# k^T v head by head in two runs of four chunks, with four slots for x^T k in borrowed space

## Chip, cores, metric

One core of one Trainium2 chip. The metric is the time of one execution in device microseconds (us). The kernel before takes 1626.18 us (median of six runs, 1625.86 to 1627.21).

## The reference

Two layers of linear attention (A) and two of a bilinear feed-forward block (B), in turn, each on a layer-normed x and added to x. x is 2048 x 1024 in bf16, with 32 heads of 32 columns. Only A matters here:

```python
q, k, v = split(x @ wqkv)                          # x is layer-normed
pq, pk = phi(q), phi(k)
kv  = einsum("bhsd,bhse->bhde", pk, v)             # one 32x32 block per head
num = einsum("bhqd,bhde->bhqe", pq, kv)
den = einsum("bhqd,bhd->bhq", pq, pk.sum(s)) + 1e-6
out = (num / den) @ wo
```

The kernel never forms v. Because kv = pk^T (x Wv), it computes G = x^T pk, an array of 1024 x 1024 in eight chunks of 128 rows ("x^T k"), and then, head by head, the 32x32 blocks of Wv^T G ("k^T v" in the kernel's words). From those blocks and wo it makes one matrix M, so that the layer's output is pq M.

## The kernel before

Chunk m of G is made in PSUM by 32 full matmuls (128x128 weights, 512 columns), ScalarE copies it to a slot in SBUF, and then 32 small matmuls, one per head, add that chunk's share to the 32 blocks in one PSUM bank. There are two slots, used in turn:

```python
Gs = [GL[:, (2 + i) * D:(3 + i) * D] for i in range(2)]

def both(ps, lhsT, rhs, start, stop):              # L199; L202 after the change
    for n in range(2):
        nc.tensor.matmul(out=ps[:, n, :], lhsT=lhsT, rhs=rhs[:, n * NB:(n + 1) * NB], ...)

def g_unit(m):                                     # x^T k, chunk m
    def run():
        for n in range(2):
            if n == 0 or m == KD - 1:
                ps = mm_tile()
            for t in range(NT):
                nc.tensor.matmul(out=ps[:, n, :], lhsT=XN[:, t, m * P:(m + 1) * P],         # L291
                                 rhs=PK[:, t, n * NB:(n + 1) * NB], start=(t == 0), stop=(t == NT - 1))
            if m == KD - 1:                        # the last chunk is copied by halves
                nc.scalar.copy(out=Gs[m % 2][:, n * NB:(n + 1) * NB], in_=ps[:, n, :])      # L294
        if m < KD - 1:
            nc.scalar.copy(out=Gs[m % 2], in_=flat(ps))                                     # L296

def kv_unit(m):                                    # k^T v, chunk m: 32 matmuls of 128x32 by 128x32
    def run():
        ...
        for h in range(2):
            for j in range(4):
                for r in range(4):
                    a = (4 * h + r) * P + j * DH
                    nc.tensor.matmul(out=acc[0][DH * r:DH * r + DH, h, j, :], lhsT=wkv[:, m, a:a + DH],
                                     rhs=Gs[m % 2][:, a:a + DH], ..., tile_position=(0, DH * r))   # L310
        if m == KD - 1:
            nc.vector.tensor_copy(out=KVb[:], in_=acc[0][:])
```

The units stand in one hand-made order; `d` is the division of one tile of q on VectorE (about 4.3 us each), `q` the q matmuls of one tile (16 full matmuls):

```python
do([g[0], g[1], z_sum, kv[0]] + d(0) + [g[2], kv[1]] + d(1, 2) + [g[3], kv[2]] + d(3) + [q[0]] + d(4))
do([g[4], kv[3]] + d(5, 6) + [q[1], g[5], kv[4]] + d(7))
load_o(0)
load_o(1)
do(d(8) + [q[2], g[6], kv[5]] + d(9, 10) + [q[3]] + d(11) + [q[4]] + d(12) + [g[7], kv[6], kv[7], q[5]])
last_q_with_m(later)
```

`last_q_with_m` makes the last two q tiles and, among their matmuls, the four quarters of M (`quarter`, L334: 16 matmuls of 32x32 weights and 512 columns). Each quarter needs KVb, a part of wo, and free PSUM banks; VectorE and ScalarE take its results out (`take`). The quarters stand eight full matmuls apart.

## Time and profile before

The first lines are those of the page for the kernel before: span, busy time, granted clock of TensorE (PE) in 40 slices, and the chain of waits that ended last.

```profile
span 1624.7 us, 18711 instructions
...
PE 1620.1 (100%) x8129; PEld 735.3 (45%) x8129; DVE 609.4 (38%) x895; ACT 287.3 (18%) x389; POOL 54.5 (3%) x136
...
PEclk9999999999999999999999999999999999999999
...
PE 100%; ACT 0%; DVE 0%; issue 0%
```

PE is the chain almost from end to end, at full clock (a mean of 1.000 granted); the ACT in it is one copy of 0.59 us in each attention layer, which comes up again below. A saving anywhere else is worth nothing unless PE waits for it. "Busy 100%" also hides what is at stake here: a full matmul's record is 0.38 us long and overlaps the next one's, so PE counts as busy through the small gaps between groups. Those gaps are read from starts, not from busy time. A full matmul starts every 0.2158 us (448 of them take 96.69 us in the chain).

Next, PE's timeline of the kernel before, around the first chunk of k^T v and then at the end of k^T v in the first layer. Columns: start, duration, engine, line, operation, output and inputs, shapes, count, and in brackets idle time before and who ended it.

```profile
104.46 0.59 PE L199 MATMUL ps<-W,ones 128*128 128x512 bf16 x2
104.98 0.38 PE L310 MATMUL kv<-GL,W 128*32 128x32 bf16 x32
105.29 7.08 PE L291 MATMUL ps<-R,R 128*128 128x512 bf16 x32
112.30 0.38 PE L310 MATMUL kv<-GL,W 128*32 128x32 bf16 x32
...
166.16 0.53 PE L310 MATMUL kv<-GL,W 128*32 128x32 bf16 x48
166.90 0.28 PE L310 MATMUL kv<-GL,W 128*32 128x32 bf16 x16 [0.21 <-ACT GL L294]
167.11 3.63 PE L199 MATMUL ps<-W,xT 128*128 128x512 bf16 x16
```

I use one measure throughout, worked out from the starts of single matmuls in the trace: the **extra time** of a trip to small matmuls and back is the start of the first full matmul after it, minus the start of the last one before it, minus 0.2158 us. For the first chunk that is 105.290 - 104.673 - 0.216 = 0.401 us. The small matmuls fill 0.200 us of it, four per 25 ns (one for each column tile, 3 to 4 ns apart; only the second four start 40 ns after the first). The other 0.20 us is going in (0.093) and out (0.108).

At the end of k^T v, chunks 6 and 7 form one trip, and the second half of chunk 7 waits for ScalarE's copy: 1.044 us extra. The chain of waits of the kernel before (start, length, what) has that copy in it:

```profile
166.24 0.02 issue
166.27 0.59 ACT GL L294
166.86 0.04 issue
166.90 0.28 PE kv L310 x16
```

Some records are missing from traces (one full matmul in about 50, in some of the profiles below); I put back one spacing where that is plain.

| per attention layer, before | us |
|---|---|
| six single chunks, 0.401 each | 2.41 |
| chunks 6 and 7 with the wait | 1.04 |
| k^T v, extra time in all | 3.45 |
| four quarters of M, 0.461 each | 1.84 |

### The profile page before, as it was taken

The numbers are of one execution on the slowest core, as the hardware profiler recorded it, in microseconds if no ns is written. First come the engines' busy times: TensorE is split into PE (matmuls) and PEld (weight loads), VectorE is DVE, ScalarE is ACT, GpSimd is POOL, SyncE is SP. The second block draws the span as 40 slices with busy tenths as digits, with TensorE's granted clock in tenths as the row PEclk, the third lists the DMA queues.
The fourth block names the chain that finished last, engine by engine and source line by source line (L and its number), as shares of the span: only waits on it lengthen the run. The fifth ranks groups of instructions, "written<-read, shape, count | busy, mean of one in ns | idle before, by whom it ended". The sixth has DMA issues, their size and how long they took to land.

```text
span 1624.7 us, 18711 instructions
## 1 busy us (share of the span) xinstructions
PE 1620.1 (100%) x8129; PEld 735.3 (45%) x8129; DVE 609.4 (38%) x895; ACT 287.3 (18%) x389; POOL 54.5 (3%) x136
## 2 busy tenths in 40 slices
PE   9999999999999999999999999999999999999999
PEld 4444444444444444444444444444444444444444
DVE  6789853212311321243245798432123113211111
ACT  5533201101110110011045222011011101101110
POOL 2100000000000000010000000000000000000000
PEclk9999999999999999999999999999999999999999
DMA  7325856511550452142420358555235406521400
GB/s 236 57 71 105 234 162 175 162 52 53 165 171 0 139 160 90 52 156 63 91 55 1 78 104 243 151 170 162 71 96 173 134 20 172 165 66 65 156 0 26
DMA packets 235937, 182.87 MB, mean 113 GB/s; under 512 B 101456, under 2 KB 216656, under 8 KB 235856
## 3 DMA queue, kind: packets, MB, share of 16 engines
q1 hardware_dynamic: 235856, 181.69, 39.2%
q8 instruction: 63, 1.03, 0.3%
q14 instruction: 18, 0.15, 0.0%
HBM read 153.09 MB, written 4.19 MB: 97 GB/s over the span
## 4 chain that ended last, share of the span: by engine, by line
PE 100%; ACT 0%; DVE 0%; issue 0%
PE ps L523 48%; PE ps L199 44%; PE ps L291 7%; PE ps L550 1%; PE kv L310 0%; PE ps L169 0%; PE pm L334 0%; PE pt L406 0%; ACT GL L294 0%; DVE xT L409 0%; DVE X L531 0%; DVE xT L164 0%; PE ps L334 0%
## 5 line engine op out<-in xcount | busy, mean ns | idle before, releaser
L523 PE MATMUL ps<-xT,R 128*128 128x512 bf16 x2432 | 528.5, 379 | 0.0
L523 PEld LDWEIGHTS <-R 128*128 128x128 bf16 x2432 | 238.0, 98 | 286.9
L527 DVE TENSOR_TENSOR R<-gs,ps 128x512 bf16<-128x512 f32 x224 | 153.8, 687 | 533.6 <-ACT gs L526 533.6
L526 ACT COPY gs<-ps 128x512 f32<-128x512 f32 x224 | 131.0, 585 | 1040.4 <-PE ps L523 1040.4
L199 PEld LDWEIGHTS <-R 128*128 128x128 bf16 x1736 | 169.9, 98 | 204.8
L523 PE MATMUL ps<-xT,W 128*128 128x512 bf16 x1152 | 251.6, 379 | 0.0
L199 PEld LDWEIGHTS <-xT 128*128 128x128 bf16 x1536 | 148.7, 98 | 178.9 <-issue 1.8
L199 PE MATMUL ps<-W,xT 128*128 128x512 bf16 x1024 | 225.3, 380 | 0.3 <-DVE xT L409 0.3
L523 PEld LDWEIGHTS <-W 128*128 128x128 bf16 x1152 | 112.7, 98 | 136.0
L199 PE MATMUL ps<-W,R 128*128 128x512 bf16 x744 | 170.7, 379 | 0.0
L531 DVE TENSOR_TENSOR X<-X,ps 128x1024 bf16<-128x1024 bf16 (+3 forms) x34 | 39.4, 1158 | 335.8 <-PE ps L199 326.1
L291 PE MATMUL ps<-R,R 128*128 128x512 bf16 x512 | 112.8, 379 | 0.0
L199 PE MATMUL ps<-PQ,R 128*128 128x512 bf16 x496 | 112.1, 379 | 0.0
L199 PE MATMUL ps<-R,xT 128*128 128x512 bf16 x512 | 110.8, 379 | 0.0
L204 ACT ACTIVATE e<-ps 128x1024 bf16<-128x1024 f32 x56 | 57.3, 1024 | 145.5 <-PE ps L199 145.5
L178 DVE BATCH_NORM_STATS2 st<-X 128x6 f32<-128x512 bf16 x128 | 81.9, 681 | 1.9 <-DMA X<-in_A_x_dram 1.8
L291 PEld LDWEIGHTS <-R 128*128 128x128 bf16 x512 | 49.8, 98 | 59.6
L182 POOL TENSOR_SCALAR ve<-mv 128x1 f32<-128x1 f32 x64 | 16.7, 260 | 1330.4 <-DVE mv L180 1330.4
L199 PE MATMUL ps<-GL,R 128*128 128x512 bf16 x248 | 58.6, 379 | 0.0
L199 PE MATMUL ps<-xT,R 128*128 128x512 bf16 x248 | 58.6, 379 | 0.0
L377 DVE TENSOR_TENSOR X<-X,ps 128x1024 bf16<-128x1024 bf16 x32 | 38.6, 1212 | 26.6 <-PE ps L199 26.6
L189 DVE TENSOR_SCALAR R<-X,mv,rstd 128x1024 bf16<-128x1024 bf16 x64 | 33.9, 542 | 23.9 <-POOL rstd L184 23.9
(64 smaller groups left out, 474.5 us busy)
## 6 DMA issues: line engine op xcount, KB each, us to landing
R<-in_B_w_gate_dram SPq DMA_DIRECT2D x38, 1024.0 KB, 5.4
R<-in_B_w_up_dram SPq DMA_DIRECT2D x38, 1024.0 KB, 7.4
W<-in_B_w_gate_dram SPq DMA_DIRECT2D x18, 1024.0 KB, 5.6
W<-in_B_w_up_dram SPq DMA_DIRECT2D x18, 1024.0 KB, 7.4
W<-in_A_wqkv_dram SPq DMA_DIRECT2D x10, 1024.0 KB, 5.9
W<-in_B_w_down_dram SPq DMA_DIRECT2D x6, 1024.0 KB, 11.5
PQ<-in_B_w_down_dram SPq DMA_DIRECT2D x4, 1024.0 KB, 7.9
X<-in_A_x_dram SPq DMA_DIRECT2D x15, 256.0 KB, 5.4
```

What stands on the lines that cost most here:

```text
L178: nc.vector.bn_stats(out=st[:, c, :], in_=X[:, t, c * NB:(c + 1) * NB])
L182: nc.gpsimd.tensor_scalar(out=ve[:], in0=mv[:, 1:2], scalar1=1e-5, scalar2=None, op0=ALU.add)
L189: nc.vector.tensor_scalar(out=dst, in0=X[:, t, :], scalar1=mv[:, 0:1], scalar2=rstd[:], op0=ALU.subtract, op1=ALU.mult)
L199: nc.tensor.matmul(out=ps[:, n, :], lhsT=lhsT, rhs=rhs[:, n * NB:(n + 1) * NB], start=start, stop=stop)
L204: nc.scalar.activation(out=e[:], in_=flat(ps), func=ACT.Exp, **sc)
L291: nc.tensor.matmul(out=ps[:, n, :], lhsT=XN[:, t, m * P:(m + 1) * P], rhs=PK[:, t, n * NB:(n + 1) * NB], start=(t == 0), stop=(t == NT - 1))
L377: nc.vector.tensor_tensor(out=X[:, t, :], in0=X[:, t, :], in1=flat(ps), op=ALU.add)
L523: nc.tensor.matmul(out=ps[:, n, :], lhsT=w[:, k, j * P:(j + 1) * P], rhs=xT[g % 2][:, k, :], start=(k == 0), stop=(k == KD - 1))
L526: nc.scalar.copy(out=gs[:], in_=ps[:, 0, :])
L527: nc.vector.tensor_tensor(out=hT[:, f, :], in0=gs[:], in1=ps[:, 1, :], op=ALU.mult)
L531: nc.vector.tensor_tensor(out=X[:, t, a:b], in0=X[:, t, a:b], in1=ps, op=ALU.add)
L550: nc.tensor.matmul(out=ps[:, 0, 0:b - a], lhsT=hT[:, f, tl * P:(tl + 1) * P], rhs=wd[f][:, a:b], start=(f == 0), stop=(f == KF - 1))
```

## The change

Its intent: gather the eight chunks, seven trips, into two trips, so that TensorE leaves its full matmuls less often, and put the second run behind a q tile, so that the last copy is covered. That takes four slots in place of two. They come from a new tile G3, from a quarter of W3 that wo fills later, and from pq[7], which is free by then but belongs to wo's second half, whose last slice can then be loaded only after the second run. x^T k also shares one lhsT between two banks, and the quarters of M move by some q matmuls.

```diff
+    G3 = const.tile([P, D], BF16, tag="G3", name="G3")
+    Gs = [GL[:, 2 * D:3 * D], GL[:, 3 * D:4 * D], G3[:], W3[:, 3 * D:4 * D]]
+    Gs += Gs[0:3] + [pq[7]]
 ... g_unit
-                for n in range(2): ...
+                ps = mm_tile()
+                for t in range(NT):
+                    both(ps, XN[:, t, m * P:(m + 1) * P], PK[:, t, :], t == 0, t == NT - 1)
+                if m == 4:
+                    kv_unit(0)()
+                nc.scalar.copy(out=Gs[m], in_=flat(ps))
 ... kv_unit(i)
+                for m in range(4 * i, 4 * i + 4):       # the 32 small matmuls as before
 ... last_q_with_m: q steps of two matmuls each, round the four quarters
-            quarter(0,0) steps(0,0,4) quarter(0,1) steps(0,4,8) quarter(1,0) steps(1,0,4) quarter(1,1) steps(1,4,8)
+            steps(0,0,2) quarter(0,0) steps(0,2,5) quarter(0,1) steps(0,5,8) steps(1,0,1)
+            quarter(1,0) steps(1,1,5) quarter(1,1) steps(1,5,8)
 ... order
-        load_o(0)
-        load_o(1)
-        do(... [g[7], kv[6], kv[7], q[5]])
+        load_o(0, 0, 4)
+        load_o(1, 0, 3)
+        do(... [g[7], q[5], kv_unit(1)])
+        load_o(1, 3, 4)
```

More of the change, by code (lines that the diff above doesn't have):

```diff
@@ L87 @@
     zhl = W3[:, 0:D]
-    Gs = [GL[:, (2 + i) * D:(3 + i) * D] for i in range(2)]
+    G3 = const.tile([P, D], BF16, tag="G3", name="G3")
+    Gs = [GL[:, 2 * D:3 * D], GL[:, 3 * D:4 * D], G3[:], W3[:, 3 * D:4 * D]]
+    Gs += Gs[0:3] + [pq[7]]
     ring = [rows(R2[:, i * KD * NB:(i + 1) * KD * NB], NB) for i in range(4)]
@@ L121, in load_q, with load_o @@
             load(wq[:, a:a + 4, :], wqkv_v[:, a:a + 4, 0:D])
-    def load_o(h):
+    def load_o(h, a, b):
         for r in range(4):
-            load(wo[h][DH * r:DH * r + DH, :, :], wo_v[h, r])
+            load(wo[h][DH * r:DH * r + DH, a:b, :], wo_v[h, r, :, a:b, :])
     def load_gu(i):
@@ L286, in run @@
             def run():
-                for n in range(2):
-                    if n == 0 or m == KD - 1:
-                        ps = mm_tile()
-                    for t in range(NT):
-                        nc.tensor.matmul(out=ps[:, n, :], lhsT=XN[:, t, m * P:(m + 1) * P],
-                                         rhs=PK[:, t, n * NB:(n + 1) * NB], start=(t == 0), stop=(t == NT - 1))
-                    if m == KD - 1:
-                        nc.scalar.copy(out=Gs[m % 2][:, n * NB:(n + 1) * NB], in_=ps[:, n, :])
@@ L295, in run, with kv_unit @@
-                if m < KD - 1:
-                    nc.scalar.copy(out=Gs[m % 2], in_=flat(ps))
+                ps = mm_tile()
[4 more added lines that the diff above has]
+                nc.scalar.copy(out=Gs[m], in_=flat(ps))
             return run
         acc = []
-        def kv_unit(m):
+        def kv_unit(i):
             def run():
-                if m == 0:
+                if i == 0:
@@ L305, in run @@
                     acc[:] = [psum.tile([P, 2, 4, DH], F32, tag="kv0", bufs=1, name="kv")]
-                for h in range(2):
-                    for j in range(4):
-                        for r in range(4):
-                            a = (4 * h + r) * P + j * DH
-                            nc.tensor.matmul(out=acc[0][DH * r:DH * r + DH, h, j, :], lhsT=wkv[:, m, a:a + DH],
-                                             rhs=Gs[m % 2][:, a:a + DH], start=(m == 0 and h == 0 and j == 0),
-                                             stop=(m == KD - 1), tile_position=(0, DH * r), skip_group_check=True)
@@ L313, in run @@
-                if m == KD - 1:
+                for m in range(4 * i, 4 * i + 4):
+                    for h in range(2):
+                        for j in range(4):
+                            for r in range(4):
+                                a = (4 * h + r) * P + j * DH
+                                nc.tensor.matmul(out=acc[0][DH * r:DH * r + DH, h, j, :], lhsT=wkv[:, m, a:a + DH],
+                                                 rhs=Gs[m][:, a:a + DH], start=(m == 0 and h == 0 and j == 0),
+                                                 stop=(m == KD - 1), tile_position=(0, DH * r), skip_group_check=True)
@@ L314, in run @@
+                if i == 1:
                     nc.vector.tensor_copy(out=KVb[:], in_=acc[0][:])
@@ L346, in last_q_with_m @@
             dve, act = nc.vector.tensor_copy, nc.scalar.copy
+            steps(0, 0, 2)
             take = quarter(0, 0, qs[1])
@@ L350, in last_q_with_m @@
             take(act, 2)
-            steps(0, 0, 4)
+            steps(0, 2, 5)
             take = quarter(0, 1, wide)
@@ L355, in last_q_with_m @@
             take(act, 2)
-            steps(0, 4, 8)
+            steps(0, 5, 8)
+            steps(1, 0, 1)
             take = quarter(1, 0, wide)
@@ L361, in last_q_with_m @@
             phi(qs[0], q_slot(14), scale_of(14), later)
-            steps(1, 0, 4)
+            steps(1, 1, 5)
             take = quarter(1, 1, wide)
@@ L367, in last_q_with_m @@
             do(later)
-            steps(1, 4, 8)
+            steps(1, 5, 8)
             phi(qs[1], q_slot(15), scale_of(15))
@@ L481, in d @@
             return [div_unit(t) for t in ts]
-        g, kv, q = ([f(i) for i in range(KD)] for f in (g_unit, kv_unit, lambda i: q_unit(8 + i)))
+        g, q = ([f(i) for i in range(KD)] for f in (g_unit, lambda i: q_unit(8 + i)))
         later = []
         q[5] = q_unit(13, later)
-        do([g[0], g[1], z_sum, kv[0]] + d(0) + [g[2], kv[1]] + d(1, 2) + [g[3], kv[2]] + d(3) + [q[0]] + d(4))
-        do([g[4], kv[3]] + d(5, 6) + [q[1], g[5], kv[4]] + d(7))
-        load_o(0)
-        load_o(1)
-        do(d(8) + [q[2], g[6], kv[5]] + d(9, 10) + [q[3]] + d(11) + [q[4]] + d(12) + [g[7], kv[6], kv[7], q[5]])
+        do([g[0], g[1], z_sum] + d(0) + [g[2]] + d(1, 2) + [g[3]] + d(3) + [q[0]] + d(4))
+        do([g[4]] + d(5, 6) + [q[1], g[5]] + d(7))
+        load_o(0, 0, 4)
+        load_o(1, 0, 3)
+        do(d(8) + [q[2], g[6]] + d(9, 10) + [q[3]] + d(11) + [q[4]] + d(12) + [g[7], q[5], kv_unit(1)])
+        load_o(1, 3, 4)
         last_q_with_m(later)
```

## The prediction

> **What bounds it.** TensorE. The page gives PE 1620.1 of 1624.7 us busy at full granted clock; the chain of waits is 100% PE. A full 128x512 matmul starts every 0.2158 us (448 in 96.69 us in the chain). Only smaller gaps in PE's stream of full matmuls save time.
>
> **What the change touches** (in both attention layers). The matmuls stay the same in number; the 256 of x^T k keep 0.2158 us with a shared lhsT, as elsewhere. What changes is how often PE leaves the full array for 128x32 tiles (k^T v).
>
> Timeline around one chunk: last full matmul starts at 104.673, the 32 small ones from 104.982 to 105.182 (four per 25 ns), the next full one at 105.290. Past normal spacing that is 0.41 us: 0.20 of small matmuls, about 0.21 of going in and out. [...]
>
> Before, per layer: six single chunks (0.41 each) and the end, where chunks 6 and 7 sit together but chunk 7's second half waits for ScalarE's copy: from 165.850 to 167.110, 1.04 us past normal spacing. From the first x^T k matmul (90.81) to the first quarter of M (170.67) pass 79.86 us, of which 354 full matmuls take 76.40: about 3.4 us to win from per layer.
>
> After: two runs of 128 small matmuls. Five fewer trips save 5 x 0.21 = 1.05 us per layer, and the wait for the last copy (0.4 us) goes, as q[5] now covers it. But I doubt that a long run keeps 25 ns per four. In the one longer run of this trace the first 32 pairs go at 6.2 ns each, later ones at about 8.4 (166.377 to 166.506). [...] Estimate for a run: 0.20 + 96 x 0.0084 + 0.21 = 1.22 us, 2.45 per layer. Saving 0.95 per layer, or 1.4 if the pace stays 6.2 ns.
>
> **New waits.** (1) KVb's cast (0.42 us) is covered only by four q matmuls; the vector engine is free at 169.2, the run ends near 169.7: it fits. (2) Quarters one and two are six matmuls apart in place of eight; DVE's two takes (1.29 us) end about 0.1 us after the second could start. (3) The last slice of wo (4 x 64 KB) can be issued only after the second run, behind tile 12's transpose (170.65); landing near 174.4, needed near 174.9: tight. Together 0.1 us per layer off.
>
> **Prediction.** 2 x 0.9 = 1.8 us saved: 1624.2 us, 1623.1 to 1625.4. Within 2%: 0.99.
>
> **What would show it.** k^T v in two stretches of about 1.0 us per layer; starts 6.2 ns apart for 32, then near 8.4; no PE idle before k^T v from a ScalarE copy; other matmuls at 0.2158; first x^T k to first quarter shorter by about 0.9 us net of the moved matmuls; little PE idle before quarters two and three.
>
> **What would make it wrong.** A run of 256 instructions uses a whole 16 KB instruction fetch (about 1 us each in the trace): if that starves, 1 us per run is lost. A late wo slice stalls quarter three. A pace of 6.2 ns gives 1 us more.

## The result, and the profile after

| | median us | runs | range |
|---|---|---|---|
| before | 1626.18 | 6 | 1625.86 to 1627.21 |
| changed | 1624.93 | 6 | 1624.50 to 1625.22 |

Ratios are the mean time of one kernel's fast runs over that of the other's of the same rounds, so not quite the ratio of the medians: here 0.9991, with a 95% interval of 0.9978 to 1.0004. By that interval alone the change is not clear of noise. The medians differ by 1.25 us and the ranges do not meet, though, and the traces show the difference step by step.

The page of the changed kernel:

```profile
span 1623.0 us, 18701 instructions
...
PE 1618.8 (100%) x8129; PEld 736.3 (45%) x8129; DVE 609.7 (38%) x895; ACT 287.4 (18%) x387; POOL 54.5 (3%) x136
...
PE 100%; DVE 0%; issue 0%
```

PE is still everything, ScalarE's copy has left the chain, and PE's busy time fell by 1.3 us. PE's timeline of the changed kernel, first layer: the first run, then the second run and the first two quarters.

```profile
128.91 0.68 PE L310 MATMUL kv<-GL,W 128*32 128x32 bf16 x64
129.42 0.45 PE L310 MATMUL kv<-G,W 128*32 128x32 bf16 x32
129.69 0.57 PE L310 MATMUL kv<-W,W 128*32 128x32 bf16 x32
130.19 3.63 PE L202 MATMUL ps<-W,xT 128*128 128x512 bf16 x16
...
164.74 3.62 PE L202 MATMUL ps<-W,xT 128*128 128x512 bf16 x16
168.28 0.66 PE L310 MATMUL kv<-GL,W 128*32 128x32 bf16 x64
168.81 0.45 PE L310 MATMUL kv<-G,W 128*32 128x32 bf16 x32
169.08 0.45 PE L310 MATMUL kv<-PQ,W 128*32 128x32 bf16 x32
169.46 1.04 PE L202 MATMUL ps<-W,xT 128*128 128x512 bf16 x4
170.42 0.39 PE L334 MATMUL pm<-W,KVb 32*32 32x512 bf16 x2
...
172.19 0.47 PE L334 MATMUL pm<-W,KVb 32*32 32x512 bf16 x2
172.29 0.39 PE L334 MATMUL ps<-W,KVb 32*32 32x512 bf16 x2
```

Read the starts. A single chunk's 32 matmuls filled 0.20 us before; here the first two chunks of a run take 0.51 to 0.53 us (128.91 to 129.42) and the next one 0.27 (129.42 to 129.69). No idle for a ScalarE copy is left. The second quarter's first matmul starts 0.10 us before the other fifteen (172.190 and 172.287 in the trace; the first line of that quarter joins two of them): its second bank was not free.

Extra time, from the starts of single matmuls:

| | before | changed |
|---|---|---|
| k^T v, first attention layer | 3.45 | 1.371 + 1.265 = 2.64 |
| k^T v, second attention layer | 3.45 | 1.357 + 1.330 = 2.69 |
| four quarters, each layer | 1.84 | 1.94 |
| first x^T k matmul to the last 512-column one | 1524.89 | 1523.40 |

The sum closes (from unrounded numbers). k^T v saves 0.82 + 0.77, the quarters give back 0.10 twice, and the second full matmul after each trip comes 0.01 us late, which ten trips fewer save: 0.82 + 0.77 - 0.20 + 0.10 = 1.49 us. The last row of the table says 1.49 (1524.89 - 1523.40). The spans differ by 1.7 us because the stretch before the first x^T k matmul was 0.24 us shorter in this profile. That stretch ends anywhere from 90.02 to 90.94 us in the profiles, in kernels that are alike up to there, so it is scatter.

### The profile page after: what moved, and what is told of

Read it like the earlier page. It is cut to its first block, busy times and chain, and to the rows that moved or that the text cites. A ratio compares the mean times of both kernels' runs of the same rounds, so it can differ in the third digit from the quotient of the medians.

```text
span 1623.0 us, 18701 instructions
## 1 busy us (share of the span) xinstructions
PE 1618.8 (100%) x8129; PEld 736.3 (45%) x8129; DVE 609.7 (38%) x895; ACT 287.4 (18%) x387; POOL 54.5 (3%) x136
## 4 chain that ended last, share of the span: by engine, by line
PE 100%; DVE 0%; issue 0%
PE ps L202 50%; PE ps L526 48%; PE ps L553 1%; PE kv L310 0%; PE ps L172 0%; PE pm L334 0%; PE pt L408 0%; DVE xT L411 0%; DVE X L534 0%; DVE xT L167 0%; PE ps L334 0%
## 5 line engine op out<-in xcount | busy, mean ns | idle before, releaser
L185 POOL TENSOR_SCALAR ve<-mv 128x1 f32<-128x1 f32 x64 | 16.7, 260 | 1328.7 <-DVE mv L183 1328.7
L278 DVE TENSOR_TENSOR tmp<-PQ,GL 128x1024 f32<-128x1024 bf16 x32 | 39.0, 1220 | 6.4 <-ACT GL L271 6.3
```

What stands on the lines that cost most here:

```text
L185: nc.gpsimd.tensor_scalar(out=ve[:], in0=mv[:, 1:2], scalar1=1e-5, scalar2=None, op0=ALU.add)
L278: nc.vector.tensor_tensor(out=tmp[:], in0=q, in1=zacc, op=ALU.mult)
```

## The experiments

Ten more runs were made, four, four and two to a chip; the kernel before, run beside them, took 1626.28, 1626.36 and 1626.38 us on the three chips. Everything that is not in an edit is as in the changed kernel. Timing alone cannot tell tenths of a microsecond apart in 1625, so the verdicts rest on extra times in the trace; the medians are given beside them.

| run | k^T v, layer one / two | quarters, one / two | first x^T k to last | median us |
|---|---|---|---|---|
| changed kernel again | 2.79 / 2.70 | 1.95 / 1.95 | 1523.56 | 1625.09 |
| pairs | 2.77 / 2.75 | 1.95 / 2.05 | 1523.75 | 1625.46 |
| quarter8 | 2.78 / 2.71 | 1.84 / 1.84 | 1523.53 | 1625.54 |
| two_heads | 2.46 / 2.46 | 3.52 / 3.52 | 1527.16 | 1628.48 |
| singles_cover | 3.09 / 3.10 | 1.94 / 2.29 | 1524.72 | 1626.17 |
| no_cover | 2.94 / 2.93 | 1.94 / 1.94 | 1523.95 | 1625.38 |
| triples | 2.76 / 2.65 | 2.08 / 1.95 | 1523.65 | 1625.36 |
| pairs_two_slots | 2.80 / 2.80 | 1.94 / 1.94 | 1523.72 | 1625.05 |

(run8 and shift16 are longer on purpose and are told below.)

### The changed kernel again

No edit.

> The changed kernel once more, beside the others on one chip. Extra time of PE past its 0.2158 us spacing, summed per attention layer: k^T v 2.6 to 2.7 us (kernel before 3.45), four quarters of M 1.94 us (before 1.84). About 1.3 us below the kernel before.

Measured: 1625.09 us against 1626.28 for the kernel before on the same chip (ratio 0.9991 again, 0.9977 to 1.0005). k^T v came to 2.79 and 2.70, a little above what I expected. The single runs took 1.34 to 1.42 us extra in this profile and 1.27 to 1.37 in the first. This sets the scatter: 0.15 us per layer.

### pairs: four runs of two chunks

```diff
-                if m == 4: kv_unit(0)()                  # chunks 0 to 3
+                if m == 2: kv_unit(0, 1)()
+                if m == 4: kv_unit(2, 3)()
+                if m == 6: kv_unit(4, 5)()
-        do(... [g[7], q[5], kv_unit(1)])                 # chunks 4 to 7
+        do(... [g[7], q[5], kv_unit(6, 7)])
```

> Four runs of two chunks in place of two of four. My theory (a trip out and back costs 0.20 us, the first 32 small matmuls 6.25 ns each [...], every later one about 8.4 ns [...]): 0.20 + 0.20 + 0.27 = 0.67 us a run, 2.7 per layer, so no change against runs of four, though there are two trips more. Rival 1 (the small matmuls are cheap at any length, the surplus seen in the long runs is a fixed loss of each run, about 0.3 us): 4 x 0.9 = 3.6 us per layer, 2 us slower in all. Rival 2 (the trips are what counts): 2 x 0.2 us more per layer, 0.8 us slower in all.

Measured: 0.686 to 0.712 us per run, 2.75 to 2.77 per layer. Theory predicted 0.67 and 2.7; rival 1 asked for 3.6 and rival 2 for 0.4 more per layer, and both fall. So a trip costs about 0.20 us. Joining two single chunks keeps over half of it (2 x 0.401 - 0.687 = 0.115 us), joining two pairs little or none (2 x 0.687 = 1.374 against 1.265 to 1.415 for a run of four). The slower pace takes about 0.07 us at each joining (32 pairs more at 8.4 in place of 6.2 ns); at the second, a pause of about 0.12 us that shift16 looks into takes most of the rest. Within a run, the starts of single matmuls show that pace: the first 32 pairs of weight load and matmul stand 6.2 to 7 ns apart, all later ones 8.3 to 8.6 ns.

One thing more came out of it. In the second layer the third quarter cost 0.10 us more: the last slice of wo landed at 981.69 us and that quarter started at 981.56. That is the "tight" wait of the prediction, in a kernel whose run ends a little differently.

### quarter8: eight matmuls between the first two quarters

```diff
-            steps(0,0,2) quarter steps(0,2,5) quarter steps(0,5,8) steps(1,0,1) quarter steps(1,1,5) quarter steps(1,5,8)
+            steps(0,0,2) quarter steps(0,2,6) quarter steps(0,6,8) steps(1,0,2) quarter steps(1,2,6) quarter steps(1,6,8)
```

> The changed kernel with eight q matmuls between the first two quarters of M, as before, in place of six (two after the last). Theory: the second quarter waits 0.10 us for VectorE's second take; here it goes at once: four quarters 1.84 us per layer in place of 1.94, 0.2 us faster in all, and no new wait at the first output tile. Rival (the wait is for the late slice of wo or for ScalarE): 1.94 stays.

Measured: the quarters are back at 1.84 us per layer, so the wait went with the two q matmuls more before the quarter. VectorE's timeline of the changed kernel shows that it was for VectorE's take, as predicted: the pair of takes ends at 170.95 + 1.29 = 172.24, and the second quarter's second bank is written from 172.29.

```profile
169.79 0.42 DVE L314 CAST KVb<-kv 128x256 bf16<-128x256 f32 x1 [1.95 <-PE kv L310]
170.95 1.29 DVE L341 CAST R<-pm 128x512 bf16<-128x512 f32 x2 [0.73 <-PE ps L334]
```

But the expectation of no new wait failed. Four full matmuls are left after the last quarter in place of six, and in both layers PE then lost 0.08 us on the way to the first output tile (0.293 us between two starts in place of 0.216, at 178.55 and 984.85). That M is what it waits for is argued from the order of the code, not shown by a named wait. Of the gain of 0.10 a layer 0.02 stays; first x^T k to last, 1523.53, is that of the changed kernel. The median is 0.45 us above it, with ranges that overlap.

### two_heads: 128x64 tiles, half the matmuls

```diff
-                        for j in range(4):
+                        for jj in range(2):
                             for r in range(4):
-                                a = (4 * h + r) * P + j * DH
-                                matmul(out=acc[0][DH*r:DH*r+DH, h, j, :], lhsT=wkv[:, m, a:a+DH], rhs=Gs[m][:, a:a+DH], ...)
+                                a, c = (4 * h + r) * P + jj * 2 * DH, r % 2 * 64
+                                matmul(out=acc[0][c:c+64, h, jj, r//2, :], lhsT=wkv[:, m, a:a+64], rhs=Gs[m][:, a:a+64], ...)
+                    # then eight copies of 32x128, four on VectorE and four on ScalarE, take out the diagonal blocks
+            steps(0,0,3) quarter steps(0,3,7) quarter steps(0,7,8) steps(1,0,3) quarter steps(1,3,7) quarter steps(1,7,8)
```

> k^T v with two heads to a tile of 128x64: 16 matmuls per chunk in place of 32, the diagonal blocks taken out by eight small copies on VectorE and ScalarE, three q steps before the first quarter to cover them, and eight q matmuls between quarters. Right result. Theory (the long run is paced by the issue of instructions, about 8.4 ns a pair): half the instructions[...]: a run of 64 takes about 0.85 us in place of 1.06 to 1.16, 1.06 with its trip, 2.1 us per layer in place of 2.66: 1.1 us less in all, 1.3 with the quarters. Rival (loading weight columns sets the pace): twice the columns per matmul, 16.7 ns a pair, no gain in the run. If the eight copies are slow, PE is idle before the first quarter.

Measured: right result, but slower: 1628.48 us, ratio 1.0014 (1.0002 to 1.0027). The run of 64 took 1.005 us and 1.228 with its trip, against 1.27 to 1.42 for 128 small ones: a gain, but half of the one expected. Two matmuls start per 31.6 ns from the first pair to the last; the 0.85 us that I expected for the run makes about 27 ns per two, an estimate that was too low. The pace is the same before and after the first 32 pairs, and no run has a pause. What sets its 15.8 ns, the array or the loading of weight columns, is not shown. It fits my reading that the slower pace of the long runs (8.3 to 8.6 ns) comes from a supply of small matmuls that runs behind the array: at 15.8 ns a matmul that supply would keep up. It does not exclude the rival (weight columns), whose 16.7 ns is near, and no run shows the supply itself.

The loss is plain in PE's timeline of two_heads; the line before it is the full matmuls after the run:

```profile
169.79 1.47 PE L202 MATMUL ps<-W,xT 128*128 128x512 bf16 x5
172.86 0.39 PE L340 MATMUL pm<-W,KVb 32*32 32x512 bf16 x2 [1.60 <-ACT KVb L318]
```

The eight copies took turns on the two engines, each waiting for the other, and ended at 172.81. That costs 1.68 us per layer in the first quarter. Another 0.51 is lost at the first output tile, and for most of it the view of waits names ScalarE's Relu of a q tile, which the copies seem to have pushed back.

### singles_cover: the cover of the last copy, without the merging

```diff
+        do([g[0], g[1], z_sum, kv(0)] + ... + [g[2], kv(1)] + ... )   # chunks 0 to 5 single, as in the kernel before
-        do(... [g[7], q[5], kv_unit(1)])
+        do(... [g[7], q[5], kv(6, 7)])
```

> Chunks 0 to 5 single as in the kernel before, 6 and 7 as one run behind the q tile, all else as in the changed kernel: the cover of the last copy without the merging. Theory: 6 x 0.40 + 0.69 = 3.1 us of k^T v per layer, against 3.45 before and 2.70 to 2.79 for the runs of four: the cover is worth 0.35 us per layer, the merging about 0.35 more. The last run ends earlier against VectorE's row of divisions, so the late slice of wo may make quarter three wait 0.1 us or so. Rival (the merging makes nearly all of it): 3.4 us.

Measured: k^T v 3.09 and 3.10, as the theory said: the cover is worth 0.36 per layer, the merging 0.30 to 0.45 more. In time the kernel is no faster than the kernel before (ratio 1.0000, 0.9988 to 1.0013), because it also takes over the change's costs: 0.10 per layer in the second quarter, and 0.35 in the third quarter of the second layer, where the last slice of wo landed at 981.73 us. PE's timeline of singles_cover there:

```profile
980.19 1.24 PE L202 MATMUL ps<-W,xT 128*128 128x512 bf16 x5
981.36 0.39 PE L332 MATMUL pm<-PQ,KVb 32*32 32x512 bf16 x2
...
981.49 0.65 PE L332 MATMUL ps<-PQ,KVb 32*32 32x512 bf16 x2
982.08 0.82 PE L202 MATMUL ps<-W,xT 128*128 128x512 bf16 x3
```

The last two of the sixteen stand 0.28 us apart (0.65 us together where the others take 0.39): the very last one, at 981.77, waited for the slice. The expected 0.1 us was too small.

### no_cover: the merging, with the last copy uncovered

```diff
-        do(... [g[7], q[5], kv_unit(1)])
+        do(... [g[7], kv_unit(1), q[5]])
```

> Two runs of four, but the second at once after the last x^T k, before the q tile: the merging without the cover. Theory: chunk 7 waits for ScalarE's copy (last x^T k start + 0.38 + 0.04 + 1.01 + 0.05 us); the run costs 1.57 us past normal spacing in place of 1.34 to 1.41, 2.95 per layer, 0.4 us slower in all than the changed kernel.

Measured: the second run costs 1.570 us in both layers, and from first x^T k to last the kernel takes 0.4 to 0.55 us more than the changed one. That is still 0.94 us less than the kernel before: the merging alone keeps most of the gain. ScalarE's and PE's timelines of no_cover:

```profile
164.68 1.01 ACT L295 CAST PQ<-ps 128x1024 bf16<-128x1024 f32 x1 [4.97 <-PE ps L202]
```

```profile
157.57 7.07 PE L202 MATMUL ps<-R,R 128*128 128x512 bf16 x32
164.57 0.66 PE L310 MATMUL kv<-GL,W 128*32 128x32 bf16 x64
165.05 0.44 PE L310 MATMUL kv<-G,W 128*32 128x32 bf16 x32
165.74 0.37 PE L310 MATMUL kv<-PQ,W 128*32 128x32 bf16 x32 [0.24 <-DVE den L280]
```

The bracket names VectorE, but the chunk's slot is filled by ScalarE, whose copy ends at 165.69; PE goes on at 165.74. A wait for several semaphores is put down to the one that came last by the profile, which here is the wrong one. After this wait the next 32 pairs start 6.3 to 6.5 ns apart, then the run is over: the wait for data brings back the pace of a single chunk (25 ns per four), as it would if, in my reading, a store of small matmuls in front of the array had filled up again meanwhile.

### triples: three runs, three slots, wo as before

```diff
-    Gs = [GL[:, 2 * D:3 * D], GL[:, 3 * D:4 * D], G3[:], W3[:, 3 * D:4 * D]]
-    Gs += Gs[0:3] + [pq[7]]
+    Gs = [GL[:, 2 * D:3 * D], GL[:, 3 * D:4 * D], G3[:]] * 3
-                if m == 4: kv_unit(0)()
+                if m == 3: kv_unit(0, 1, 2)()
+                if m == 6: kv_unit(3, 4, 5)()
-        load_o(1, 0, 3) ... [g[7], q[5], kv_unit(1)]) ... load_o(1, 3, 4)
+        load_o(1, 0, 4) ... [g[7], q[5], kv_unit(6, 7)])
-            steps(0,0,2) quarter steps(0,2,5)
+            steps(0,0,1) quarter steps(0,1,5)
```

> Runs of three, three and two chunks with three slots only, so that no slot lies in wo's space and wo loads as in the kernel before; one q step before the first quarter of M and eight q matmuls between quarters. Theory: runs of 96 stay short of the pause: 0.20 + 0.20 + 64 x 0.0084 = 0.94 us, twice, and 0.69: 2.6 us per layer against 2.70 to 2.79; quarters 1.84 against 1.95; no wait for KVb, wo or M. About 0.5 us below the changed kernel, 1.9 below the kernel before. Rival (three trips are dearer than two): 2.9 us of k^T v per layer, no gain.

Measured: 2.76 and 2.65, no gain to speak of. Three of the runs of 96 cost 0.979, near the 0.94 expected, but the fourth had a pause of 0.113 us already after pair 68, so "runs of 96 stay short of the pause" falls. And one q step of two matmuls is too little before the first quarter: PE waited there for KVb.

```profile
169.12 0.66 PE L311 MATMUL kv<-GL,W 128*32 128x32 bf16 x64
169.71 0.61 PE L201 MATMUL ps<-W,xT 128*128 128x512 bf16 x2
170.48 0.39 PE L335 MATMUL pm<-W,KVb 32*32 32x512 bf16 x2 [0.16 <-DVE KVb L315]
```

The first quarter cost 0.23 and 0.11 us more in the two layers, more than the 0.10 per layer that the wider spacing had won. From the last small matmul's start to the first quarter passed 0.75 and 0.88 us here, where two matmuls and the two switches cover 0.65 (0.116 + 0.226 + 0.309).

### run8: all eight chunks in one run

```diff
-    Gs += Gs[0:3] + [pq[7]]
+    Gs += pq[4:8]
-                if m == 4: kv_unit(0)()
-        load_o(1, 0, 3)
-        do(... [g[7], q[5], kv_unit(1)])
-        load_o(1, 3, 4)
+        do(... [g[7], q[5], kv_unit(*range(8))])
+        load_o(1, 0, 4)
```

> All eight chunks in one run of 256 small matmuls after the last-but-two q tile; the whole second half of wo then loads late, so the third quarter of M will wait some us on purpose: only the run itself is read. Theory (past the first 32 pairs the issue of instructions sets about 8.4 ns a pair, and where the long runs of four show a pause of 0.11 to 0.13 us late in the run, the supply of instructions has run dry): 0.20 + 0.20 + 224 x 0.0084 = 2.28 us, and two to six pauses of 0.12, so 2.5 to 3.0 us: no better than two runs of four (2.70 to 2.79), though it makes one trip less. Rival (the pauses are chance, or belong to the slots' semaphores): 2.3 to 2.4 us.

The result is wrong: the first half of wo was loaded over the slot of chunk 3 before the run had read it. No wait of the program depends on values, so the run's timing can still be read. It was 1631.94 us (1631.23 to 1635.39), with the late half of wo and the stop told below in it.

In the second layer the run cost 2.42 us, with one pause of 0.115 us at pair 218 and one of 0.084 at pair 95, where chunk 3 begins (pairs are counted from 0, and a pause follows the pair named). That is between the two expectations. In the first layer it cost 4.62 us, because PE stood still for more than two microseconds in mid-run. PE's timeline of run8:

```profile
167.72 0.77 PE L308 MATMUL kv<-PQ,W 128*32 128x32 bf16 x71
170.66 0.49 PE L308 MATMUL kv<-PQ,W 128*32 128x32 bf16 x44 [2.18 <-issue]
171.09 1.45 PE L202 MATMUL ps<-W,xT 128*128 128x512 bf16 x3
```

"issue" means that the profile shows nothing PE waited for. A fetch of instructions (one 16 KB packet) was under way from 168.23 to 169.29, which fits the fear of the prediction that a long run can outrun the fetch. But the 32 pairs after the stop go at 6.2 ns, the pace of a run's first 32 pairs, and not at 8.3. In my reading, then, instructions had arrived before PE went on; the fetch had ended 1.4 us earlier. The cause of this stop stays open; it was profiled once.

The stop settles something else. A chunk is 32 small matmuls, so in all other runs of these tiles the slower pace could begin at pair 32 because a chunk ends there, and not because 32 pairs had gone by, whatever their chunk. Here the stop came 20 pairs into chunk 6. The fast pace then held for 32 pairs, across the start of chunk 7, and the slow one came back 20 pairs into chunk 7. So the count runs from the last standstill, and the ends of chunks have no part in it.

### pairs_two_slots: runs of two in the two old slots

```diff
-    G3 = const.tile([P, D], BF16, tag="G3", name="G3")
-    Gs = [GL[:, 2 * D:3 * D], GL[:, 3 * D:4 * D], G3[:], W3[:, 3 * D:4 * D]]
-    Gs += Gs[0:3] + [pq[7]]
+    Gs = [GL[:, 2 * D:3 * D], GL[:, 3 * D:4 * D]] * 4
 ... runs as in pairs, wo loaded whole as in the kernel before
```

> Four runs of two chunks in the two slots of the kernel before: no new tile, no slot in wo's space, wo loaded as before; quarters as in the changed kernel. Theory: 4 x 0.687 = 2.75 us of k^T v per layer, quarters 1.94, no wait for wo: as fast as the changed kernel within 0.2 us (its k^T v is 2.64 to 2.79), without its extra space. Rival (the slots of the change are needed, ScalarE's copies would wait for a run or a run for a copy): waits of about 1 us at the runs, 3.5 us or more per layer.

Measured: right result, 1625.05 us against 1626.38 for the kernel before on the same chip, ratio 0.9992 (0.9978 to 1.0006). k^T v 2.80 in both layers, quarters 1.94, no wait for wo. By the trace the stretch is 0.15 to 0.31 us longer than in the changed kernel's two profiles, and by the clock equal. PE's timeline of pairs_two_slots, first layer, shows the first two runs with full matmuls on both sides and no wait for a copy:

```profile
112.02 0.68 PE L311 MATMUL kv<-GL,W 128*32 128x32 bf16 x64
112.63 7.08 PE L199 MATMUL ps<-R,R 128*128 128x512 bf16 x32
...
130.00 0.68 PE L311 MATMUL kv<-GL,W 128*32 128x32 bf16 x64
130.61 1.25 PE L199 MATMUL ps<-W,xT 128*128 128x512 bf16 x5
```

A run of two needs two slots, so the new tile, the borrowed quarter of W3, pq[7] and the split load of wo buy nothing that shows.

### shift16: where do the pauses come from?

```diff
-            idle(9)
+            idle(25)
```

> The changed kernel with 16 idle matmuls more at the very start, so that every later instruction of TensorE stands 32 places further on in its program; about 3 us longer on purpose. If the short pauses in the long runs (pairs 113, 124, 113 and 94 to 98 of the four runs in the changed kernel's profiles) belong to places in the program, as in a supply of instructions by blocks, they come 16 pairs earlier: near 97, 108, 97 and 80. If they belong to what is done in the run or to the time since it began, they stay where they are.

In the runs of four, one place per run (in two profiles of the second run two places, close together) has a pause of 0.08 to 0.17 us that no wait explains; only one run of the first profile had none (a gap of 0.05 us instead). Across the changed kernel again, quarter8 and the first profile these places hardly move: pair 113, pair 124 to 126, pair 112 to 114, pair 92 to 98. With every instruction 32 places further on, they are at pairs 113, 126, 112 and 92: they did not move. So they are not tied to a place in the program, and the supply of instructions in fixed blocks is ruled out as their cause. The traces agree: in these four profiles no instruction fetch of 16 KB was under way during any of the pauses (the nearest began at 939.79 us in shift16, after a pause that ended at 939.75). After such a pause the pace is still 8.3 ns, so, if the reading of a store is right, it did not fill meanwhile, and something ahead of it stopped. What it was stays open.

## Why the prediction was right, and where it was off

- **What bounds the kernel.** Right: PE is the whole chain before and after, and the saving seen in the stream of full matmuls (1.49 and 1.33 us) is the saving in time (1.25 and 1.19 us by the medians) to within 0.25 us.
- **A single chunk costs 0.41 us, 0.21 of it going in and out.** Right: 0.401, and 0.01 more at the second matmul after it. pairs and singles_cover show the same cost of a trip.
- **"Chunk 7's second half waits for ScalarE's copy", and q[5] covers it.** Right: the wait is gone. no_cover brings it back and costs 0.4 to 0.55 us in all.
- **A long run does not keep 25 ns per four.** Right: 32 pairs near 6.2 ns, then 8.3 to 8.6. no_cover and run8 show that a standstill brings back 32 fast pairs, run8 that the end of a chunk does not set the count. Every long run of 128x32 tiles in this case turns at pair 32. That 32 pairs stand in store when a run begins is inferred from that number alone. That the issue of instructions then sets the 8.3 ns is my reading of the even spacing (weight loads, too, start 8 to 9 ns apart in the changed kernel's trace); no run measures the issue by itself.
- **"Estimate for a run: ... = 1.22 us".** This is the term that was mis-sized. The runs cost 1.27 to 1.42: a pause of about 0.12 us in nearly every run of four, and 0.02 to 0.04 near pair 63 in most of them, were not foreseen. The four runs together came to 5.32 us in the first profile where I had 4.9. That 0.4 us is more than the whole difference between the 1.8 us predicted and the 1.49 found in the trace; the two terms that I left out, 3.45 in place of 3.4 before and 0.01 us at each trip's second matmul, go the other way, by 0.1 us each. The 1.8 itself was rounded up: 2 x (0.95 - 0.1) is 1.7. The range of 1623.1 to 1625.4 allowed any saving from 0.8 to 3.1 us, so that the time fell into it says little; the terms above say more.
- **KVb fits behind four q matmuls.** Right, with 0.2 us to spare in the first layer (the cast ends at 170.21, the quarter starts at 170.42); triples shows that two are not enough.
- **Up to 0.1 us lost at the second quarter.** Right: 0.098 in each layer, and quarter8 shows that it is VectorE's takes.
- **The last slice of wo is tight.** Right for the changed kernel: it landed at 173.84 us and the third quarter started at 174.49. In the second layer of pairs and of singles_cover it came too late, by up to 0.35 us: its loads went out 1.25 us later than in the changed kernel (from 977.20 and 977.19 us in place of 975.94), the quarter started only 0.6 to 0.8 us later.
- **Instruction fetch could starve a run of 256.** Not seen in runs of four. In the traces before and after, 63 fetches of 16 KB each took 0.88 to 1.56 us, with a median of 256 weight loads and matmuls from one to the next. run8 has one stop of two microseconds that could be that or not.

From the first x^T k matmul to the last 512-column one, the merging alone saves 0.94 us (no_cover) and both together 1.33 to 1.49; with the cover alone the change's own costs (second quarter, late wo) ate the gain (0.17 us in the trace; 1626.17 against 1626.36 us). A version clearly better than the changed kernel was not found; the same gain with half the slots was.

## What to carry to other kernels

When an engine is the whole chain, look for its gain in the starts of its instructions, not in busy time: here about 0.2 us for each of 14 trips and two waits of about 0.36 us were all that this change could reach. Joining groups of tiny matmuls saves trips, but longer runs go at a slower pace (8.3 to 8.6 ns a pair after the first 32, which take 6.2 to 7 each) and met pauses (0.08 to 0.17 us), so the gain flattens after the first joining: with the last copy covered in all, 3.09 us per layer with six single chunks, 2.75 to 2.80 in pairs, 2.64 to 2.79 in fours. Before borrowing space for a larger grouping, try the smallest one; and whenever a stage gets shorter, check which loads and copies were hidden behind it.
